# A long convolution and a soft mixture of experts in one kernel: the transform's first stage in 60 and 30 columns, its spectra stored by frequency, and a step's work put in another order

## The chip, the cores and the metric

The kernel runs on one core of one Trainium2 chip. The metric is device time in microseconds, the median of several executions. Times inside the kernel come from one execution that was recorded by the hardware profiler.

## The reference

All data is float32. `x` holds 8 sequences of 5696 tokens by 128 channels, `h` one filter of the same length. The first block is a causal convolution per channel by a Fourier transform of twice the length; the second block is a soft mixture of experts on the 45568 tokens that come out.

```python
Xf = np.fft.rfft(x, n=2*S, axis=1); Hf = np.fft.rfft(h, n=2*S, axis=0)
y = np.fft.irfft(Xf * Hf[None], n=2*S, axis=1)[:, :S, :].reshape(B*S, D)
logits = y @ phi                                  # 32 slots: 8 experts of 4
d = np.exp(logits - logits.max(0)); d /= d.sum(0) + 1e-9
slot_input = (d.T @ y).reshape(8, 4, 128)
slot_out[e] = np.maximum(slot_input[e] @ w1[e], 0) @ w2[e]
c = np.exp(logits - logits.max(1, keepdims=True)); c /= c.sum(1, keepdims=True) + 1e-9
out = c @ slot_out
```

## The kernel before, in words

The transform is split as 90 times 64 (N1 = 90, N2 = 64). A sequence is 89 rows (R1) of 64 tokens. For the filter and then each of the 8 sequences (g = 0 for the filter, 9 in all) the kernel walks through 8 steps (NJ); step c handles four tokens of the first half of each row and the four that mirror them, so there are 72 steps (NA) in which new data is transformed. All the work of all stages is put in one sequence of steps t, written out by hand; each engine, and SP, which issues nearly all DMAs, runs its own instructions in just that order.

**First stage.** `load_x` brings a step's tokens to a tile `xc` (two DMAs, 80 and 9 rows, in pieces of 2 KB); three such tiles are in rotation. `fold` adds or subtracts the mirrored tokens on POOL (L202; component 0 is the sum, 1 the difference). `stage_a(t, comp)` multiplies each of these by a table of 90 frequencies, spread over 128 columns: one matmul for the real and one for the imaginary part (L213), each into a PSUM bank, each copied by ACT into a tile `fst` (L215). Two DMAs of 45 frequencies each write `fst` to the spectrum `f` in DRAM (L219), whose layout is (half, token n, frequency q, re/im, channel), so in pieces of 1 KB. A step has four such matmuls and four such DMAs. The program's float32 matmul shows as two records in the profile.

**Second stage and back.** A unit is four of the 45 frequency rows (the last unit of a sequence is one); 12 units to a sequence, one in an odd step t and two in an even one. `load_g` reads a unit's spectra into a tile `gt` (L237; 128 rows of 4 KB). `stage_b1` transforms them over the 64 tokens into the PSUM tile `bt` (L251; two banks, one buffer); DVE multiplies by the filter's spectrum there (L269, L278); `stage_b2` transforms back into the PSUM tile `bz` (L293; two banks), ACT copies it (L298), SP writes it to `z` in DRAM (L301). `slot_b` runs `stage_b1` of a fresh unit and then `stage_b2` of the unit before it.

**Tokens and experts.** Every second step a pair T begins: `load_pair` reads `z` into the one tile `zc` (L329, five DMAs, rows of 16 KB), at the start of the even step before the pair's own. In the odd step `stage_c1` does the last stage of the inverse transform (L348) with `stage_c4` (L414 to L430) between its halves, and later `stage_c5` and `softmax`; in the even step come `stage_c2` (transposes, L376), `stage_c6`, `stage_c3` (logits, L385), `dispatch` (L461) and `column_max`. `pair(lag)` says which pair's stage falls in step t. The units of a sequence begin 9 steps, its pairs 27 steps after its first step.

**Rings.** All stages but b take their PSUM banks from one ring of four (`bank()`); a bank comes free when ACT or DVE has copied it. The other four banks are `bt` and `bz`. SP issues its DMAs in program order and waits at each until its data and its buffer are ready.

Order of an even step before: `load_pair`, `prefetch(t + 1)`, `load_x(t + 3)`, `stage_a(t, 0)`, fold, `dispatch`, unit, c2, c6, `stage_a(t, 1)`, fold, c3, unit, `column_max`. Order of an odd one: `prefetch(t + 1)`, `load_x(t + 3)`, `stage_a(t, 0)`, fold, c1 with c4, unit, c5, `stage_a(t, 1)`, fold, softmax. At the first step of a sequence `prefetch` comes later, after the middle unit.

After step 72 the first stage is over, and w1 is loaded; after the units end, `front` is closed and the last pairs run with eight banks. Then come the experts and the product with the output weights.

Of the kernel before, what the change touches and what calls it, by code (L numbers as in the profile page):

```python
# [10 lines left out]
F32 = mybir.dt.float32  # L11
AF = mybir.ActivationFunctionType
# [8 lines left out]
    return [(0, 64, 32, 1)] + left  # L21


def transform_tables(S, N1, N2, CH, X0, F0, F1):

# [16 lines left out]
    i1 = np.stack([np.cos(a0), -np.sin(a0), -np.cos(a0)], 1)  # L44
    NP = N1 // 2
    part = s1
    s1 = np.zeros((P, 3, P))
    for a, p in enumerate((F0, F1)):
        s1[X0:X0 + R1, :, p:p + NP] = part[:, :, a * NP:(a + 1) * NP]
    part = i1[np.arange(N1).reshape(2, NP).T.reshape(-1)]  # L50
    i1 = np.zeros((P, 3, N2))
    for r, n, p, step in z_blocks(N1):
# [23 lines left out]
def kernel(  # L76
# [25 lines left out]
    P = 128  # L102
# [15 lines left out]
    NQ = NJ // 2  # L118
    assert S == R1 * N2 and R1 == N1 - 1 and D == P and CH == Q == 4
    SPLIT = R1 // 16 * 16  # L120
    X0, F0, F1 = 20, 6, 82
    ctx.enter_context(tc.manual_schedule())

    t_s1, t_i1, t_w, t_v, t_turn = [
        nc.inline_tensor(t, f"tab_{n}").ap()
        for n, t in zip(("s1", "i1", "w", "v", "turn"), transform_tables(S, N1, N2, CH, X0, F0, F1))]
    fd = [nc.dram_tensor(f"f_{g}", (2, N2, NP, 2, D), F32, kind="Internal").ap() for g in range(B + 1)]
    zd = [nc.dram_tensor(f"z_{b}", (NP, 2 * N2, 2, D), F32, kind="Internal").ap() for b in range(B)]
    cd = nc.dram_tensor("c_t", (P, B * NQ, Q, 2, MH), F32, kind="Internal").ap()

# [28 lines left out]
    apool = lead.enter_context(tc.tile_pool(name="apool", bufs=2, side="right"))  # L159
    bpool = front.enter_context(tc.tile_pool(name="bpool", bufs=1))  # L160

    s1 = apool.tile([P, 3, P], F32, name="s1", tag="s1", bufs=1)
    wt = fconst.tile([P, NP, HP], F32, name="wt")
    vt = fconst.tile([P, NU, 2, HP], F32, name="vt")
    turn = fconst.tile([P, 2, NW, 2, 2], F32, name="turn")
# [3 lines left out]
    def bank():  # L169
        rings.append(rings.pop(0))  # L170
        return rings[-1].tile([P, 512], F32, name="bank", tag="bank")


    xs = {}
    xf = [apool.tile([P, CH, D], F32, name=f"x{i}", tag=f"x{i}", bufs=1) for i in range(2)]
    xcs = [apool.tile([P, 2, CH, D], F32, name=f"xc{i}", tag=f"xc{i}", bufs=1) for i in range(3)]
    for t_ in xcs:
        nc.vector.memset(t_[:, :, :, :], 0.0)

    def load_x(c):  # L180
        if c >= (B + 1) * NJ:
            return
        g, j = divmod(c, NJ)
        src = (h if g == 0 else x[g - 1]).rearrange("(a n) d -> a n d", n=N2)
        t_ = xcs[c % len(xcs)]
        gap = N2 - CH * (2 * j + 1)
        for r in (slice(0, SPLIT), slice(SPLIT, R1)):
            v = src[r, CH * j:CH * (j + 1), :]
            v = bass.AP(tensor=v.tensor, offset=v.offset,
                        ap=[v.ap[0], [gap * D, 2], [1, CH * D]])  # L190
            nc.sync.dma_start(
                out=t_[X0 + r.start:X0 + r.stop, :, :, :].rearrange("p s n d -> p s (n d)"), in_=v)
        xs[c] = t_

    folded = {}

    def fold(c, comp):
        if c not in xs:
            return
        t_ = xs.pop(c) if comp else xs[c]  # L200
        y_ = xf[comp]
        nc.gpsimd.tensor_tensor(out=y_[:, :, :], in0=t_[:, 0, :, :], in1=t_[:, 1, ::-1, :],  # L202
                                op=AL.subtract if comp else AL.add)
        folded[(c, comp)] = y_

    def stage_a(c, comp):
        g, j = divmod(c, NJ)
        src = folded.pop((c, comp))
        tab = (0, 1) if comp == 0 else (1, 2)
        st = apool.tile([P, CH, 2, D], F32, name="fst", tag="fst", bufs=5)  # L210
        for G in range(2):
            p = bank()
            nc.tensor.matmul(p[:, :], s1[:, tab[G], :],  # L213
                             src[:, :, :].rearrange("p n d -> p (n d)"), start=True, stop=True)
            nc.scalar.activation(st[:, :, G, :],  # L215
                                 p[:, :].rearrange("p (n d) -> p n d", d=D), AF.Copy)
        n0 = comp * HALF + CH * j
        for a, p in enumerate((F0, F1)):
            nc.sync.dma_start(  # L219
                out=fd[g][a, n0:n0 + CH, :, :, :].rearrange("n q c d -> q n (c d)"),  # L220
                in_=st[p:p + NP, :, :, :].rearrange("k n c d -> k n (c d)"))


    gs, prods = {}, {}

# [5 lines left out]
    def load_g(u):  # L231
        if u >= (B + 1) * NW:
            return
        g, w, us = parts(u)
        n = sum(k for _, k in us)
        t_ = bpool.tile([P, 4, 2, D], F32, name="gt", tag="gt", bufs=3)
        nc.sync.dma_start(  # L237
            out=t_[:, 0:n, :, :].rearrange("p q c d -> p (q c d)"),
            in_=fd[g].rearrange("a r q c d -> (a r) (q c d)")[:, 8 * w * D:(8 * w + 2 * n) * D])
        gs[u] = t_  # L240

    def stage_b1(u, share):
        g, w, us = parts(u)
        t_ = gs.pop(u)
        tag = "bz" if g == 0 and w % 2 else "bt"
        bt = bps.tile([P, 2, 2, 2 * D], F32, name="bt", tag=tag)
        for o, (i, n) in enumerate(us):
            for a in range(2):
# [9 lines left out]
        else:  # L258
            pv = bt[r, :, 0, :].rearrange("p a (c d) -> p a c d", c=2)
        k = 2 * m  # L260
        pi = bpool.tile([P, 4, 2, D], F32, name="p", tag="pi", bufs=2)
        for p_, H_ in ((pi[r, 0:k, :, :], turn[:, 1] if g == 0 else Hi), (pv, turn[:, 0] if g == 0 else Hr)):
            if g:
                h_ = H_[r, w].rearrange("p a o d -> p (a o) d") if m == 2 else H_[r, w, :, 0]
# [17 lines left out]
    def stage_b2(u):  # L282
        g, w, us = parts(u)
        if g == 0:
            return
        m = len(us)
        y_ = prods.pop(u)
        bz = bps.tile([P, 2, 2, 2 * D], F32, name="bz", tag="bz")
        for o, (i, n) in enumerate(us):
            for q in range(n):  # L290
                r = slice(q * HP, (q + 1) * HP)
                for a in range(2):
                    nc.tensor.matmul(bz[a * HP:(a + 1) * HP, q, o, :], vt[r, i, a, :],  # L293
                                     y_[r, a * m + o, :, :].rearrange("p c d -> p (c d)"),
                                     start=True, stop=True)
        n = us[0][1]
        st = bpool.tile([P, 2, 2, 2 * D], F32, name="zst", tag="zst", bufs=3)
        nc.scalar.activation(st[:, 0:m, 0:n, :].rearrange("p o q x -> p q o x"),  # L298
                             bz[:, 0:n, 0:m, :], AF.Copy)
        k = m * n  # L300
        nc.sync.dma_start(  # L301
            out=zd[g - 1][4 * w:4 * w + k, :, :, :].rearrange("q r c d -> r q (c d)"),
            in_=st[:, :, :, :].rearrange("p o q x -> p (o q) x")[:, 0:k, :])
# [243 lines left out]

    load_x(0)
    nc.scalar.dma_start(out=s1[:, :, :], in_=t_s1)
    for c in range(1, 3):  # L550
        load_x(c)
    nc.sync.dma_start(out=wt[:, :, :], in_=t_w)
    nc.sync.dma_start(out=vt[:, :, :, :], in_=t_v)
    nc.scalar.dma_start(out=phi[:, :], in_=moe_phi)
# [2 lines left out]
    for comp in range(2):  # L557
        fold(0, comp)
    wait_b2 = []

    for t in range(last_front + 1):
        us = list(units(t))

        def pair(lag):
            T, half = divmod(t - LAG_C - lag, 2)
            return T if half == 0 and 0 <= T < NT else None
# [4 lines left out]
                load_g(queue[loaded][0])  # L571
                loaded += 1

        turns = {2: (1, 3), 1: (2,)}.get(len(us), ())

        def slot_b(place=None):
            if place is not None and place not in turns:
                return
            fresh = bool(us)
            if fresh:  # L580
                u = us.pop(0)
                stage_b1(u, t < LAG_C or t >= NA)
                wait_b2.append(u)
            if len(wait_b2) > fresh:
                stage_b2(wait_b2.pop(0))

        if pair(-1) is not None:
            load_pair(pair(-1))
        if t % NJ:
            prefetch(t + 1)  # L590
        if t < NA:
            load_x(t + 3)
            stage_a(t, 0)
            fold(t + 1, 0)
        if pair(3) is not None:
            dispatch(pair(3))
        if t < last_front:
            slot_b(1)
        T, U = pair(0), pair(2)
        if t == last_front:  # L600
            assert T is None and U is None
            slot_b()
            slot_b()
            stage_c2(pair(1))
            slot_b()
            assert not us and not wait_b2
            V = pair(1)
            stage_c6(V - 2)
            stage_c3(V)
            column_max(V)  # L610
            break
        rows = (lambda: None) if U is None else (lambda: stage_c4(U))
        after = None
        if T is not None:
            after = stage_c1(T, rows)
        else:
            rows()
        if pair(1) is not None:
            stage_c2(pair(1))
        if pair(5) is not None:  # L620
            stage_c6(pair(5))
        if after:
            after()
        slot_b(2)
        if t % NJ == 0:
            prefetch(t + 1)
        if U is not None:
            stage_c5(U)
        if t < NA:
            stage_a(t, 1)  # L630
            fold(t + 1, 1)
        if pair(1) is not None:
            stage_c3(pair(1))
        slot_b(3)
        if pair(1) is not None:
            column_max(pair(1))
        if U is not None:
            softmax(U)
        if t == NA:
            lead.close()  # L640
            wts = inner.enter_context(tc.tile_pool(name="wts", bufs=1, side="right"))
# [221 lines left out]
```

## Time and profile before

| | |
|---|---|
| median of 6 runs | 898.47 us (895.01 to 903.22) |
| profiled execution, its time | 900.75 us |
| its span | 899.0 us |
| granted TensorE clock, mean | 0.949 |
| busy: PE, DVE, ACT, POOL | 808.3, 644.6, 480.9, 405.3 us |
| DMA moved | 272.44 MB in 156967 packets, mean 303 GB/s |
| DMA packets of the main queue | 90.3% of 16 engines' span |

Windows of the profile give each engine's busy time in a stretch of the span. A DMA share near 1.00 says that the time that all packets took, summed, is that of 16 engines busy all the time; packets overlap a little, so it can be above 1. The chain is the work that ended last, followed back: the engine and line named at each step is the one that all later work waited for.

### The profile page before, as it was taken

Reading aid. Unit: us, or ns where it says so; the run is one execution under the profiler, and the core shown is the slowest. Engines: PE = TensorE matmul, PEld = TensorE weight load, DVE = VectorE, ACT = ScalarE, POOL = GpSimd, SP = SyncE. Lnnn points to the kernel's source line nnn. Section 1 sums busy time; section 2 is a strip of 40 time slices with the busy share of each in tenths; the row PEclk is TensorE's granted clock in tenths of the full one; section 3 lists DMA queues with packets and bytes.
Section 4 is the critical chain, followed back from the end, with each engine's and each line's share of the span. In section 5 each row is a group of like instructions: output and inputs, shape, how many; then the busy total and the mean of one; then the engine's idle time right before and its main releaser. Section 6 shows DMA issues by size and latency. Waiting matters only on the chain.

```text
span 899.0 us, 19379 instructions
## 1 busy us (share of the span) xinstructions
PE 808.3 (90%) x7220; PEld 423.3 (47%) x7220; DVE 644.6 (72%) x928; ACT 480.9 (53%) x888; POOL 405.3 (45%) x385
## 2 busy tenths in 40 slices
PE   6959888789999999999999999999988877978893
PEld 2323334344445444544455555444544444445783
DVE  3039776676878888888888888777787987873542
ACT  4624344455655665666665666656653444683441
POOL 4624333244555555555555555555533343681000
PEclk9979999999999999999999999999999998988865
DMA  9989999999999999999999999999987986770898
GB/s 291 265 248 333 291 324 334 338 331 311 296 319 330 331 307 322 332 313 316 327 318 315 323 324 318 311 308 320 314 282 245 324 283 243 295 279 17 308 406 329
DMA packets 156967, 272.44 MB, mean 303 GB/s; under 512 B 12182, under 2 KB 114838, under 8 KB 153733
## 3 DMA queue, kind: packets, MB, share of 16 engines
q1 hardware_dynamic: 156299, 270.85, 90.3%
q8 instruction: 58, 0.95, 0.4%
q10 hardware_dynamic: 576, 0.36, 0.2%
q14 instruction: 34, 0.28, 0.1%
HBM read 142.86 MB, written 128.21 MB: 302 GB/s over the span
## 4 chain that ended last, share of the span: by engine, by line
PE 72%; DMA 17%; issue 3%; SPq 2%; DVE 2%; ACT 2%; POOL 1%; DVEq 0%; ACTq 0%; POOLq 0%
PE bank L213 25%; PE bank L348 12%; PE bt L251 11%; PE bz L293 8%; DMA gt<-f 5%; PE bank L376 5%; DMA out_dram<-o 4%; PE bank L461 3%; DMA zc<-z 3%; PE bank L385 2%; PE bank L437 2%; PE bank L414 2%; DMA f<-fst 1%; PE bank L485 1%; SPq L329 1%
## 5 line engine op out<-in xcount | busy, mean ns | idle before, releaser
L202 POOL TENSOR_TENSOR x<-xc 128x512 f32<-128x512 f32 x144 | 183.2, 1274 | 240.4 <-PE bank L213 183.0
L213 PE MATMUL bank<-x,s 128*128 128x512 f32 x576 | 276.3, 616 | 9.4 <-POOL x L202 9.3
L215 ACT ACTIVATE fst<-bank 128x512 f32<-128x512 f32 x288 | 171.6, 597 | 94.6 <-PE bank L213 79.6
L298 ACT ACTIVATE zst<-bz 128x1024 f32<-128x1024 f32 x96 | 93.3, 972 | 192.1 <-PE bz L293 172.4
L269 DVE TENSOR_TENSOR p<-bt,Hi 128x1024 f32<-128x1024 f32 x96 | 113.0, 1177 | 103.3 <-PE bt L251 102.9
L213 PEld LDWEIGHTS bank<-x,s 128*128 128x128 f32 x576 | 102.7, 193 | 127.9 <-issue 94.6
L251 PE MATMUL bt<-gt,wt 64*64 64x256 f32 x1620 | 116.7, 396 | 34.6 <-DMA gt<-f 17.4
L348 PE MATMUL bank<-zc,i 128*64 128x512 f32 x480 | 118.5, 617 | 7.6 <-DMA zc<-z 5.4
L278 DVE TENSOR_TENSOR yf<-bt,p 128x512 f32<-128x512 f32 x192 | 119.4, 663 | 3.3
L269 DVE TENSOR_TENSOR bt<-bt,Hr 128x1024 f32<-128x1024 f32 x96 | 113.0, 1178 | 0.0
L251 PEld LDWEIGHTS bt<-gt,wt 64*64 64x64 f32 x1620 | 55.3, 134 | 111.7 <-issue 58.2
L293 PE MATMUL bz<-yf,vt 64*64 64x256 f32 x1440 | 102.4, 382 | 0.0
L367 POOL TENSOR_TENSOR y<-y,op 128x512 f32<-128x512 f32 x64 | 77.4, 1210 | 7.9 <-DVE op L353 5.2
L293 PEld LDWEIGHTS bz<-yf,vt 64*64 64x64 f32 x1440 | 60.6, 135 | 21.9 <-issue 0.6
L367 POOL TENSOR_TENSOR y<-y,om 128x512 f32<-128x512 f32 x54 | 64.0, 1185 | 2.1
L348 PEld LDWEIGHTS bank<-zc,i 128*64 128x64 f32 x480 | 30.3, 138 | 69.1 <-issue 48.6
L422 POOL MEMSET dt<- 64x8 f32 x32 | 3.4, 107 | 123.0 <-issue 63.1
L376 PE MATMUL bank<-ident,y 109*128 109x109 f32 x512 | 57.7, 268 | 0.7 <-DVE y L367 0.7
L376 PEld LDWEIGHTS bank<-ident,y 109*128 109x128 f32 x512 | 51.2, 146 | 12.3 <-POOL L L450 6.6
L378 ACT ACTIVATE yt<-bank 128x360 f32<-128x360 f32 x128 | 50.1, 481 | 1.4 <-PE bank L376 1.4
L269 DVE TENSOR_TENSOR p<-bt,turn 128x1024 f32<-128x1024 f32 (+1 forms) x12 | 14.1, 1173 | 51.0 <-PE bt L251 50.9
L816 PE MATMUL op<-so,cT 32*128 32x128 f32 x704 | 45.8, 373 | 5.2 <-ACT o L825 4.7
(97 smaller groups left out, 856.3 us busy)
## 6 DMA issues: line engine op xcount, KB each, us to landing
f<-fst SPq DMA_DIRECT2D x288, 180.0 KB
gt<-f SPq DMA_DIRECT2D x99, 512.0 KB
z<-zst SPq DMA_DIRECT2D x88, 512.0 KB
zc<-z SPq DMA_DIRECT2D x30, 1024.0 KB
xc<-in_x_dram SPq DMA_DIRECT2D x64, 320.0 KB
out_dram<-o SPq DMA_DIRECT2D x16, 1024.0 KB
zc<-z SPq DMA_DIRECT2D x90, 128.0 KB
out_dram<-o SPq DMA_DIRECT2D x8, 768.0 KB
```

The lines of the kernel that those rows point to most:

```text
L202: nc.gpsimd.tensor_tensor(out=y_[:, :, :], in0=t_[:, 0, :, :], in1=t_[:, 1, ::-1, :], op=AL.subtract if comp else AL.add)
L213: nc.tensor.matmul(p[:, :], s1[:, tab[G], :], src[:, :, :].rearrange("p n d -> p (n d)"), start=True, stop=True)
L215: nc.scalar.activation(st[:, :, G, :], p[:, :].rearrange("p (n d) -> p n d", d=D), AF.Copy)
L251: nc.tensor.matmul(bt[q * HP:(q + 1) * HP, a, o, :], wt[r, 2 * i + q, :], t_[r, 2 * o + q, :, :].rearrange("p c d -> p (c d)"), start=True ...
L269: nc.vector.tensor_tensor(out=p_, in0=pv, in1=h_, op=AL.mult)
L278: eng.tensor_tensor(out=y_[r, 0:k, c, :], in0=pv[:, :, c, :], in1=pi[r, 0:k, 1 - c, :], op=op_)
L293: nc.tensor.matmul(bz[a * HP:(a + 1) * HP, q, o, :], vt[r, i, a, :], y_[r, a * m + o, :, :].rearrange("p c d -> p (c d)"), start=True, sto ...
L298: nc.scalar.activation(st[:, 0:m, 0:n, :].rearrange("p o q x -> p q o x"), bz[:, 0:n, 0:m, :], AF.Copy)
L348: nc.tensor.matmul(p[h_ * HP:(h_ + 1) * HP, :], i1[0:kr, tab, :], t_[0:kr, h_, o, :, q, :], start=True, stop=True)
L367: eng.tensor_tensor(out=part_, in0=part(v, 0), in1=o_[:, :, :], op=sign)
L376: nc.tensor.transpose(p[:, i * TR:(i + 1) * TR], ys[T][0:TR, k * CH + i, 0:D], ident[0:TR, 0:TR])
L378: nc.scalar.activation(yt[:, k * CH:(k + 1) * CH, :, :], of_tokens(p), AF.Copy)
```

## The change

The first stage's 90 frequencies, now ordered by q and half, are cut into 60 and 30. `first_low(c)` computes the first 60 of both components of a step in one bank: two matmuls of 64 columns, one beside the other in the output partitions, for each of the real and imaginary parts. `first_high(c)`, in odd steps alone, computes the last 30 of both components of two steps: four matmuls of 32 columns in a bank, again for each part. Each result is copied and stored: two DMAs of 60 rows from `first_low`, four of 30 rows from `first_high`. The spectrum `f` is now laid out (frequency q, half, token n, re/im, channel), so that a store's pieces are 4 KB, 64 KB apart; `load_g` reads four q of 128 rows in pieces of 1 KB.

`load_x` loads two steps at a time in pieces of 4 KB, into two tiles of twice the size; the folded tiles are four instead of two. `bt` has two buffers, which take all of the four banks outside the ring; `stage_b2` takes two banks of the ring, copied by two ACT instructions. `gt` has four buffers (three before), `fst` four (five before), `pi` one (two before). The order of a step is now a string of letters:

```diff
-    fd = [... (2, N2, NP, 2, D) ...]
+    fd = [... (NP, 2, N2, 2, D) ...]
...
-    xf = [apool.tile([P, CH, D], F32, ...) for i in range(2)]
-    xcs = [apool.tile([P, 2, CH, D], F32, ...) for i in range(3)]
+    xf = [apool.tile([P, CH, D], F32, ...) for i in range(4)]
+    xcs = [apool.tile([P, 2, 2 * CH, D], F32, ...) for i in range(2)]
...
-    def stage_a(c, comp):
-        st = apool.tile([P, CH, 2, D], F32, name="fst", tag="fst", bufs=5)
+    def first_stage(tiles, width):
+        st = apool.tile([P, CH, 2, D], F32, name="fst", tag="fst", bufs=4)
         for G in range(2):
             p = bank()
-            nc.tensor.matmul(p[:, :], s1[:, tab[G], :],
-                             src[:, :, :].rearrange("p n d -> p (n d)"), start=True, stop=True)
+            for o, (c, comp) in enumerate(tiles):
+                k = slice(0, HP) if width == HP else slice(HP, HP + QP)
+                nc.tensor.matmul(p[o * width:(o + 1) * width, :], s1[:, comp + G, k],
+                                 folded[(c, comp)][:, :, :].rearrange("p n d -> p (n d)"),
+                                 start=True, stop=True)
             nc.scalar.activation(st[:, :, G, :],
                                  p[:, :].rearrange("p (n d) -> p n d", d=D), AF.Copy)
-        for a, p in enumerate((F0, F1)):
+        for o, (c, comp) in enumerate(tiles):
+            g, j = divmod(c, NJ)
+            n0 = comp * HALF + CH * j
+            k0, n = (0, N1A) if width == HP else (N1A, N1 - N1A)
             nc.sync.dma_start(
-                out=fd[g][a, n0:n0 + CH, :, :, :].rearrange("n q c d -> q n (c d)"),
-                in_=st[p:p + NP, :, :, :].rearrange("k n c d -> k n (c d)"))
+                out=fd[g].rearrange("q a r c d -> (q a) (r c d)")[k0:k0 + n, n0 * 2 * D:(n0 + CH) * 2 * D],
+                in_=st[o * width:o * width + n, :, :, :].rearrange("k n c d -> k (n c d)"))
+    def first_low(c):
+        first_stage([(c, comp) for comp in range(2)], HP)
+    def first_high(c):
+        both = [(c - 1 + i, comp) for i in range(2) for comp in range(2)]
+        first_stage(both, QP)
...
-        t_ = bpool.tile([P, 4, 2, D], F32, name="gt", tag="gt", bufs=3)
+        t_ = bpool.tile([P, 4, 2, D], F32, name="gt", tag="gt", bufs=4)
         nc.sync.dma_start(
-            out=t_[:, 0:n, :, :].rearrange("p q c d -> p (q c d)"),
-            in_=fd[g].rearrange("a r q c d -> (a r) (q c d)")[:, 8 * w * D:(8 * w + 2 * n) * D])
+            out=t_[:, 0:n, :, :].rearrange("p q c d -> p q (c d)"),
+            in_=fd[g][4 * w:4 * w + n, :, :, :, :].rearrange("q a r c d -> (a r) q (c d)"))
...
-        tag = "bz" if g == 0 and w % 2 else "bt"
+        tag = f"bt{u % 2}"
...
-        bz = bps.tile([P, 2, 2, 2 * D], F32, name="bz", tag="bz")
+        bz = [bank() for _ in range(us[0][1])]
...
-        nc.scalar.activation(st[:, 0:m, 0:n, :].rearrange("p o q x -> p q o x"),
-                             bz[:, 0:n, 0:m, :], AF.Copy)
+        for q in range(n):
+            nc.scalar.activation(st[:, 0:m, q, :],
+                                 bz[q][:, 0:m * 2 * D].rearrange("p (o x) -> p o x", o=m), AF.Copy)
...
+    ORDER_E, ORDER_O, XAHEAD = "XYf1wb5s", "zXfb26dPxb3m", 4
...
+            "z": lambda: load_pair(pair(-1)) if pair(-1) is not None else None,
+            "x": lambda: load_x(t + XAHEAD) if t < NA else None,
+            "P": lambda: prefetch(t + 2),
+            "X": lambda: first_low(t) if t < NA else None,
+            "Y": lambda: first_high(t) if t < NA and t % 2 else None,
+            "f": lambda: [fold(t + 1, comp) for comp in range(2)] if t < NA else None,
+            "d": lambda: dispatch(pair(3)) if pair(3) is not None else None,
+            "b": lambda: slot_b(),
...
+        for c_ in (ORDER_E if t % 2 else ORDER_O):
+            work_[c_]()
```

`1` is c1 with c4 between its halves and `w` its second part; 2, 6, 5 and 3 are c2, c6, c5 and c3; `m` is `column_max`, `s` softmax. So `ORDER_E` is that of odd steps t, `ORDER_O` that of even ones: all units' spectra of two steps and x of two steps are loaded in the middle of the even step.

## The prediction

> **What bounds the kernel now.** The page's busy line says PE 808.3 of 899.0 us, its queue line that packets fill 90.3% of 16 DMA engines. Two resources that close need stages told apart, so the windows came next:
>
> ```profile
> core 0: us, PE busy (x) PEld busy (x) DVE busy (x) ACT busy (x) POOL busy (x), PEclk, DMA share, GB/s
> 0.00:50.00 50.00, 35.91 (x76) 14.03 (x76) 7.24 (x8) 23.55 (x39) 27.14 (x28) 1.00 0.91 276
> 110.00:200.00 90.00, 78.40 (x640) 38.15 (x632) 62.11 (x71) 45.09 (x67) 32.05 (x26) 1.00 1.01 330
> 149.00:171.00 22.00, 17.06 (x127) 8.66 (x128) 13.23 (x18) 9.89 (x15) 6.93 (x6) 1.00 1.02 336
> 200.00:660.00 460.00, 456.28 (x4037) 227.18 (x4040) 371.33 (x535) 278.13 (x508) 251.00 (x234) 1.00 0.97 318
> ```
>
> From 200 to 660 us (steps 27 to 72, all stages running) PE is busy 456.28 of 460 us, DMA at 0.97. What a full DMA looks like stands in the row above: 1.02, 336 GB/s, while PE idles a fifth of the time. So the middle is bound by PE with DMA about 5% behind, and the lead from 110 us on by DMA. The chain, over a period of two steps in the middle, is PE without a gap:
>
> ```profile
> 415.87 1.91 PE bank L213 x4
> 417.78 1.87 PE bank L348 x8
> 419.64 0.59 PE bank L414 x4
> 420.23 1.87 PE bank L348 x8
> 422.10 1.04 PE bt L251 x16
> ...
> 424.14 3.43 PE bank L213 x8
> ...
> 432.59 1.81 PE bank L213 x4
> 434.40 0.74 PE bank L385 x8
> ```
>
> and in the lead it runs through loads and stores of the spectrum:
>
> ```profile
> 148.97 6.88 DMA gt<-f
> 155.86 4.78 DMA f<-fst
> 160.72 5.97 DMA gt<-f
> ```
>
> A batch of eight steps takes 85.5 us in the middle (starts of the x8 piece, 338.60 to 424.14). I work per batch; the middle has 460 / 85.5 = 5.4 of them, the DMA-bound part of the lead 90 to 150 us, taken as 2.
>
> **PE.** Removed: eight full matmuls per period, 3.43 + 1.81 + 1.91 = 7.15 us. Added: `first_low` twice, which is two pairs of 64 columns each; that is exactly the shape of L348 (128*64, 512 columns, x8), 1.87 us, so 3.74. And `first_high`, two groups of four 32-column matmuls. No such group with 512 columns is in the trace. The nearest row is L385, four of 32 columns side by side, 360 columns long, 0.74 us: scaled by length 1.05 us a group; from below, a group can't beat a full matmul's 3.43 / 4 = 0.86. I take 1.0, as fill and drain don't scale. Together 5.74; saved 1.4 a period (1.3 to 1.7), 5.6 a batch: PE's floor is 79.9 us (78.7 to 80.3).
>
> The Trainium skill ("TensorE: Matmul & The Clock Gate", Measured speedup vs the span model) speaks against part of this: four tiles packed in rows gave 3.07 times, not 4. By that, an estimate, a group costs 1.12 us, the two 0.25 us more a period than I take. The sum keeps the value scaled from L385's row, which is this kernel's own.
>
> **DMA.** The trace's packet records between 300 and 600 us have means of 50 ns (1 KB), 110 (2 KB), 204 (4 KB), 725 (16 KB); the commonest times are 46, 84, 159, 611. The rest sits on the first packets of a DMA on each engine, and mostly on loads: 45 ns a packet for `gt`, 26 for `xc`, 4 for stores. Per batch, in packets times ns:
> - before: xc 1424 x 110, f 5760 x 50, z 5760 x 50, gt 1408 x 204 + 128 x 50, zc 360 x 725, c 512 x 64, others 12 us: 1335 us, / 16 = 83.4, that is 0.975 of 85.5, as the window says.
> - xc in half the DMAs and 4 KB pieces: 712 x 159 plus half the excess (18) = 132 us instead of 157: -25.
> - f stored in 4 KB: 1440 x 159 plus the same excess (24) = 253 instead of 288: -35.
> - gt read in 1 KB: 5760 x 46 plus the excess. It belongs to a DMA's start, and there are as many DMAs of as many bytes, so 63 us: 328 instead of 294: +34. If it belonged to the packet (45 each), 524: +230.
>
> Sum -26, / 16 = -1.6: 81.8 us of packets a batch. At 1.02 that is 80.2 us, at 0.975 it is 83.9.
>
> A rule of the skill speaks against the stores. "DMA: Bandwidth & Descriptors", Latency and other measured facts, says that a row pitch of large powers of two slows HBM, 207 GB/s at 512 KiB; the new stores have 64 KB, below its table. By an estimate at 207 GB/s the 5.9 MB of f a batch would take 28 us instead of 16. The trace has a row for the pitch: `zc` is read in rows 64 KB apart, and 611 ns for 16 KB (27 GB/s an engine) is its commonest packet time; it shows no such loss, for reads.
>
> **What else moves.** ACT: six copies of `fst` instead of eight (0.60 each), but `zst` in two of 0.60 instead of one of 1.03: -1.2 + 0.5 a period, with ACT busy 278 of 460: nothing. DVE keeps 371 of 460, at most 0.88 of a batch of 79 us: nothing, but it is close behind. `bt` with two buffers takes away the 1.06 us "issue" gaps before L251 in the lead (two a period); there DMA is the bound, so what is late next is the spectra: nothing. `bz` in the ring: 25 banks a period pass through four instead of 21. The slowest release is `dispatch`'s bank, copied by DVE behind a unit's 3.8 us (2 x 1.22 + 2 x 0.69); four allocations and about 2.9 us of PE follow (a unit's two halves and L385), and in the step's order DVE is done before: nothing, at worst 0.5 us a period. `pi` has one buffer, written and read by DVE alone: nothing. `xc` for two steps at the start doubles the first load: +1 us.
>
> SP's order: an even step now issues zc (5 DMAs), two stores of f, z, c, then three gt and two xc, then z; an odd one six stores of f and one z. Behind the five big loads wait only the last z and the odd step's stores; `zst` has three buffers and `fst` four, one period's worth or more, so their lateness is covered by up to a period. The gt loads are issued some 8 us before the first is needed and take 6.7 from issue to landing now: covered, without much to spare. But demand is uneven: about 5.5 MB in the even step (zc 1.5, gt 1.6, z 1.0, xc 0.7, f 0.5, c 0.2) and 1.5 in the odd one, where 336 GB/s carry 3.5 in a step's 10.4 us. The 2.0 MB left over plus the odd step's 1.5 are 10.4 us of work: DMA just stays busy, if SP issues early enough. I take a share of 1.00: 81.8 us a batch, PE's floor being 1.9 below.
>
> **Sum.** Middle: (85.5 - 81.8) x 5.4 = -20 us. Lead: 2 batches x 1.6 = -3; the first 50 us run PE-bound (x48 of L213 in 23 us) at share 0.91, of which I give back 4 us, less 1 for the first load. The last 240 us keep their work. 900.75 - 26 = 874.7; the profiled execution stands 2.3 above the median: **872 us**. Ends of this case: PE's floor of 79.9 and a lead 12 better, 5.4 x 5.6 + 12 = 42: 856; share 0.975, 8.6 + 3: 887.
>
> **Rivals.**
> 1. *The bunched loads let DMA run dry.* In the odd step SP has only stores, which PE paces. If the share falls to 81.8 / 85.5 = 0.957, the middle gains nothing and PE waits instead, seen as DMA gt or zc on the chain: about 893 to 898. For it: share 0.97 now, with an order that spreads loads over both steps. Against it: the work left over from the even step fills the odd one, by the sum above.
> 2. *Slower: the 1 KB reads cost by the packet.* Place: gt<-f in the lead and the middle. Row: xc's packets of 2 KB carry 26 ns each. At 46 + 26 = 72, gt takes 415 us instead of 294: with -60 of the others +61, / 16 = +3.8: 87.2 a batch at share 1.00, which is +1.7 x 5.4 = 9, and +7.6 in the lead, where it counts whole: 915. At 45 ns it would be 94 a batch and over 960. It decides from about 21 ns a packet, where packets fill 85.5. Stores slowed by their pitch would act the same way. For it: loads show nearly all the excess. Against: within a DMA, packets after the first run at the commonest time.
> 3. *Four tiles don't run together*, so the change doesn't save PE time: `first_high` would cost 8 x 0.86 = 6.9 a period instead of 2, 3.5 more than before. L385's 0.74 us rules it out.
>
> **Numbers.** Forecast 0.62, all of it faster; rival 1 0.15 (0.06 faster, 0.09 same); rival 2 and its like 0.23, slower. Faster 0.68, same 0.09, slower 0.23; the line between is 0.5% (4.5 us), about what a measurement of this kernel can tell from no change. Range: 856, PE's floor, to 912, into the second rival; its far bound stays outside with most of its chance.
>
> **What the profile after would show.** L213 with 64 and 32 columns, near 3.7 + 2.0 us a period on PE; a batch near 82 us; DMA share at or above 1.00 from 200 to 660 us with about 330 GB/s, and PE there at some 0.97, its waits named gt, zc or a bank. The mean of 1 KB packets below 55 ns. The "issue" gaps before L251 gone. It would be wrong if the share between 200 and 660 us falls below 0.96, if 1 KB packets go over 65 ns or 4 KB stores far over 170, or if PE's time per batch doesn't drop by 5 us.

## The result and the profile after

The changed kernel takes 895.41 us (median) where the kernel before took 899.72 in the same comparison: a ratio of 0.9954, 95% interval 0.994 to 0.9967. That is 0.5% faster where 2.9% (872 us) was forecast: inside the stated range (856 to 912), but about a sixth of the gain. Its profiled execution took 897.89 us, span 896.1.

PE's relief came as worked out. The windows of the changed kernel, in the columns shown before:

```profile
core 0: us, PE busy (x) PEld busy (x) DVE busy (x) ACT busy (x) POOL busy (x), PEclk, DMA share, GB/s
0.00:50.00 50.00, 32.29 (x138) 8.65 (x138) 8.04 (x7) 16.69 (x27) 25.39 (x27) 1.00 0.85 270
110.00:200.00 90.00, 69.55 (x672) 28.48 (x664) 58.91 (x68) 35.39 (x63) 28.41 (x24) 0.94 1.00 312
200.00:660.00 460.00, 435.26 (x4450) 202.66 (x4444) 353.53 (x540) 259.35 (x536) 252.94 (x234) 1.00 0.98 322
```

PE's busy time between 200 and 660 us fell from 456.28 to 435.26, but it now idles 25 us there; DMA share rose only from 0.97 to 0.98. In the lead DMA moves 312 GB/s at share 1.00, where it was 330 at 1.01.

Where the time went, by the start of each pair's c1 (the first matmul of L348, now L367, in the trace): the first pair starts at 190.1 us instead of 180.9, so the lead lost 9. The 22 pairs from there take 466 us instead of 473.5, a gain of 7 where 20 was forecast: a batch is 84.7 us, not 82 (pairs 4 to 20; 85.8 before by this count). What follows gains 4 to 5 more, where nothing was forecast; no run takes that apart.

The lead's 9 us have two parts. The first unit of spectra reaches PE 1.7 us later than before (56.1 us instead of 54.4), and from there to the first pair it takes 134.0 us instead of 126.5. In the first part the chain before was PE alone, six steps in 23 us:

```profile
8.05 23.08 PE bank L213 x48
```

After the change the first fold starts 2.7 us later (9.46 instead of 6.73 us), and PE and POOL take turns, two steps in 8.9 us instead of 7.7, as `first_high` reads the folded tiles of two steps and POOL refills them behind it:

```profile
9.46 1.27 POOL x L208
10.78 7.60 PE bank L219 x32
19.59 3.72 POOL x L208 x3
23.36 3.91 PE bank L219 x22
```

The chain of the changed kernel, in the middle, says how PE's time turned into a wait:

```profile
414.01 0.43 PE bank L395 x4
414.44 6.91 DMA zc<-z
...
421.41 0.35 SPq L515
...
421.82 6.08 DMA gt<-f
427.90 0.04 issue
427.94 1.09 PE bt L269 x16
```

L515 is c's store in `stage_c6`. It doesn't need zc. The trace never shows more than eight of these DMAs between issue and landing, and each uses one of eight completion semaphores in turn, so a DMA is issued only once the eighth before it has landed; SP waits there, and all behind it waits. Here z's five DMAs, two stores of f and one of z hold all eight places. The chain runs from z's load, over c's store that had to wait for the first of z's DMAs to land, to the spectra that SP could issue only then, to PE.

The other half of the same picture is SP's own row of time (start, duration of issue, line, count):

```profile
462.13 0.35 SPq L515 DMA_DIRECT2D c_t<-cst  x1
462.70 3.47 SPq L255 DMA_DIRECT2D gt<-f  x3
466.26 0.86 SPq L196 DMA_DIRECT2D xc<-in_x_dram  x2
467.22 0.60 SPq L320 DMA_DIRECT2D z<-zst  x1
467.91 8.03 SPq L228 DMA_DIRECT2D f<-fst  x6
476.39 0.39 SPq L320 DMA_DIRECT2D z<-zst  x1
476.96 3.56 SPq L348 DMA_DIRECT2D zc<-z  x5
```

The six stores of f take SP 8.03 us: the last three, whose data are ready, go out only as two of the loads of spectra and one of x ahead of them land. SP's waits from 200 to 660 us add that up:

```profile
SPq L228 <- DMA gt<-f: 70.9, 50, 2.8
SPq L228 <- DMA xc<-in_x_dram: 33.6, 21, 2.1
SPq L515 <- DMA zc<-z: 30.8, 19, 3.4
```

Before the change the largest such wait of f's stores for a DMA was 35.0 us (for zc).

In the lead, where there is no z to load yet, the spectra of the next steps wait behind such stores:

```profile
103.89 2.56 SPq L255 DMA_DIRECT2D gt<-f  x3
106.55 1.16 SPq L196 DMA_DIRECT2D xc<-in_x_dram  x2
107.80 9.58 SPq L228 DMA_DIRECT2D f<-fst  x8
117.48 0.58 SPq L320 DMA_DIRECT2D z<-zst  x1
118.16 2.88 SPq L255 DMA_DIRECT2D gt<-f  x3
```

From 50 to 200 us f's stores wait 37.5 us for spectra to land (26 times).

### The profile page after: what moved, and what is told of

It is laid out like the page before. It is cut to its first block, busy times and chain, and to the rows that moved or that the text cites. A ratio compares the mean times of both kernels' runs of the same rounds, so it can differ in the third digit from the quotient of the medians.

```text
span 896.1 us, 20345 instructions
## 1 busy us (share of the span) xinstructions
PE 767.0 (86%) x7796; PEld 376.7 (42%) x7796; DVE 622.0 (69%) x927; ACT 441.1 (49%) x904; POOL 403.1 (45%) x385
## 3 DMA queue, kind: packets, MB, share of 16 engines
q8 instruction: 62, 1.02, 0.5%
## 4 chain that ended last, share of the span: by engine, by line
PE 43%; DMA 37%; DVE 10%; issue 3%; SPq 2%; POOL 2%; ACT 1%; DVEq 0%; POOLq 0%; ACTq 0%
DMA zc<-z 11%; DMA gt<-f 11%; PE bank L219 10%; PE bank L367 7%; PE bt L269 7%; DMA f<-fst 6%; PE bank L311 5%; PE bank L395 4%; DMA out_dram<-o 4%; DMA xc<-in_x_dram 3%; PE bank L480 2%; DVE yf L296 2%; DVE p L287 2%; DVE bt L287 2%; PE op L823 2%
## 5 line engine op out<-in xcount | busy, mean ns | idle before, releaser
L208 POOL TENSOR_TENSOR x<-xc 128x512 f32<-128x512 f32 x144 | 179.4, 1271 | 244.2 <-PE bank L219 224.9
L219 PE MATMUL bank<-x,s 128*32 128x512 f32 (+1 forms) x1152 | 219.1, 613 | 17.7 <-POOL x L208 17.0
L317 ACT ACTIVATE zst<-bank 128x512 f32<-128x512 f32 (+1 forms) x184 | 98.7, 586 | 203.9 <-PE bank L311 195.0
L222 ACT ACTIVATE fst<-bank 128x512 f32<-128x512 f32 x216 | 127.5, 598 | 115.1 <-PE bank L219 87.1
L367 PE MATMUL bank<-zc,i 128*64 128x512 f32 x480 | 117.5, 611 | 21.4 <-DMA zc<-z 13.9
L311 PE MATMUL bank<-yf,vt 64*64 64x256 f32 x1440 | 102.2, 388 | 25.0 <-DVE yf L296 24.7
L219 PEld LDWEIGHTS bank<-x,s 128*32 128x32 f32 (+1 forms) x1152 | 53.8, 124 | 149.9 <-issue 80.0
L311 PEld LDWEIGHTS bank<-yf,vt 64*64 64x64 f32 x1440 | 57.2, 136 | 55.3 <-issue 30.0
L372 DVE TENSOR_TENSOR y<-bank,y 128x512 f32<-128x512 f32 x32 | 22.1, 691 | 80.3 <-PE bank L367 80.1
L367 PEld LDWEIGHTS bank<-zc,i 128*64 128x64 f32 x480 | 31.8, 137 | 85.1 <-issue 50.4
L395 PE MATMUL bank<-ident,y 109*128 109x109 f32 x512 | 63.7, 275 | 0.7 <-DVE y L386 0.7
L395 PEld LDWEIGHTS bank<-ident,y 109*128 109x128 f32 x512 | 53.4, 149 | 16.6 <-issue 10.8
L441 POOL MEMSET dt<- 64x8 f32 x32 | 3.4, 106 | 111.7 <-issue 69.4
L287 DVE TENSOR_TENSOR p<-bt,turn 128x1024 f32<-128x1024 f32 (+1 forms) x12 | 14.2, 1180 | 56.1 <-PE bt L269 55.5
```

The source lines that it names most:

```text
L208: nc.gpsimd.tensor_tensor(out=y_[:, :, :], in0=t_[0], in1=t_[1], op=AL.subtract if comp else AL.add)
L219: nc.tensor.matmul(p[o * width:(o + 1) * width, :], s1[:, comp + G, k], folded[(c, comp)][:, :, :].rearrange("p n d -> p (n d)"), start=Tr ...
L222: nc.scalar.activation(st[:, :, G, :], p[:, :].rearrange("p (n d) -> p n d", d=D), AF.Copy)
L287: nc.vector.tensor_tensor(out=p_, in0=pv, in1=h_, op=AL.mult)
L311: nc.tensor.matmul(bz[q][a * HP:(a + 1) * HP, o * 2 * D:(o + 1) * 2 * D], vt[r, i, a, :], y_[r, a * m + o, :, :].rearrange("p c d -> p (c ...
L317: nc.scalar.activation(st[:, 0:m, q, :], bz[q][:, 0:m * 2 * D].rearrange("p (o x) -> p o x", o=m), AF.Copy)
```

## The experiments

Theories at the start: A, DMA was already nearly full in the middle, so relief of PE buys little; B, the new layout of f costs DMA what PE gained; C, not bytes but SP's order and its eight places bind. Theory D, named in e9, is C in the lead.

**e1: PE's relief alone.** The imaginary part of the difference is left out; its copy takes the real part's bank.

```diff
 # kernel before, stage_a
-            p = bank()
-            nc.tensor.matmul(p[:, :], s1[:, tab[G], :], ...)
+            if G == 0 or comp == 0:
+                p = bank()
+                nc.tensor.matmul(p[:, :], s1[:, tab[G], :], ...)
```

> The kernel before with three first-stage matmuls a step instead of four (the imaginary part of the difference is not computed; its copy takes the real part's bank again): PE's relief alone, 1.8 us a period of two steps, with the same ACT copies, DMAs and order. Theory A (the middle's DMA is already nearly full, so relief of PE buys little): 4 to 12 us faster than before, the DMA share between 200 and 660 us at 0.98 to 1.00, PE no longer without gaps. Theory B (the change's own DMAs, 4 KB stores and 1 KB loads, ate the gain): PE's relief pays in full here, 25 to 35 us faster, a batch of eight steps near 79 us.

Measured: 886.38 us, 0.986 of before (0.9815 to 0.9906), a batch of 83.6 us.

```profile
200.00:660.00 460.00, 431.29 (x4079) 219.68 (x4078) 377.63 (x555) 276.00 (x521) 256.60 (x238) 1.00 0.98 326
```

That is A's range at its upper end, or just above it: with the old order, the old layout and one buffer for `bt`, a quarter of the first stage's matmuls is worth 13 us, and then DMA is at 0.98 and PE idles 29 us. A "full" DMA is 0.98 in the middle, not 1.00. But relief alone also beat the whole change, so the change takes something back.

**e2: the layout alone.** The kernel before with the spectrum stored by frequency:

```diff
-    fd = [... (2, N2, NP, 2, D) ...]
+    fd = [... (NP, 2, N2, 2, D) ...]
-                out=fd[g][a, n0:n0 + CH, :, :, :].rearrange("n q c d -> q n (c d)"),
+                out=fd[g][:, a, n0:n0 + CH, :, :].rearrange("q n c d -> q (n c d)"),
```

> The kernel before with the spectrum stored by frequency, nothing else: stores of 45 rows in 4 KB pieces 128 KB apart, loads in 1 KB pieces. In this kernel 4 KB packets are nearly all stores of f, and 2 KB are x, so their means can be told apart. Theory A: within 4 us of before, a store's 4 KB packet well under 190 ns on the mean. Theory B: 8 to 20 us slower, most of it in the lead before 200 us; 4 KB packets over 190 ns or 1 KB over 55 ns.

Measured: 896.81 us, 1.0002 (0.9962 to 1.0042). In the middle 1 KB packets, half of them now loads, took 51.2 ns on the mean (50.2 before), 4 KB packets, nearly all stores, 184 ns. All packets of a batch come to 82.8 us, 1.1 less than before the change in the same count. B falls, and with it the forecast's second rival. The Trainium skill's rule on row pitches of large powers of two ("DMA: Bandwidth & Descriptors", Latency and other measured facts) does not bite here: the pitch in this run is 128 KB, below its table. In that row 207 GB/s at 512 KiB stands beside a full rate of 214, so the row itself shows hardly any loss at that pitch, and the forecast's 28 us were no price for it. The changed kernel's own pitch, 64 KB, also ran in e9: 181 ns for a 4 KB packet.

**e3 and e5: half the spectra, after and before.** Two of a unit's four frequency rows are loaded, the rest of the tile holds zeros; as many DMAs, 2.9 MB a batch less.

```diff
-        t_ = bpool.tile([P, 4, 2, D], F32, name="gt", ...)
+        t_ = gts[u % 4]          # u % 3 in e5; set to zero at the start
+        n = (n + 1) // 2
```

> The changed kernel with half of each unit's spectra loaded (two of four frequency rows; the other half of the tile holds zeros from the start): 2.9 MB a batch of 27 less, in as many DMAs. Theory A (bytes bound it): 25 to 45 us faster than the changed kernel, a batch near PE's 79 to 80 us, DMA share falling to 0.90 to 0.95. Rival C (not bytes but SP's order and the number of DMAs in flight bind it): under 12 us faster, share falling with the bytes to about 0.89.

> The kernel before with half of each unit's spectra loaded, as in e3: the control. Theory A (before, the middle is PE's; after, it is DMA's): the middle keeps its batch of 85.5 us within 0.5 us, only the lead and the steps after the first stage gain, so 3 to 15 us faster than before, against 38 in e3. Rival (DMA set the pace of the middle before, too): 25 us or more faster, as in e3.

Measured: e3 857.55 us, 0.9534 of before (0.9505 to 0.9564), 38 us faster than the changed kernel; e5 885.64 us, 0.9884 (0.9829 to 0.9938). From 300 to 600 us, e3 and then e5:

```profile
300.00:600.00 300.00, 298.58 (x3055) 137.82 (x3057) 241.19 (x373) 179.18 (x371) 176.24 (x165) 1.00 0.92 304
```

```profile
300.00:600.00 300.00, 300.00 (x2654) 149.44 (x2654) 245.51 (x353) 184.24 (x338) 167.06 (x155) 1.00 0.90 286
```

e3 is bound by PE again, a batch of 80.6 us: this is the floor, forecast at 79.9. e5's batch is 85.5, before the change 85.8. So the middle was PE's before and is DMA's after, as forecast. What DMA makes of it isn't bytes alone, though: e3 also shortens every wait for a landing.

**e4: x ahead of the spectra.** `ORDER_O = "zXfb26dxPb3m"`.

> The changed kernel with the load of x one place earlier, ahead of the three loads of spectra. If x waiting in SP's queue behind spectra that wait for the stores of the step before is what lengthens the lead: the first pair's start comes 4 to 8 us earlier (190 us now, 181 before the change) and the kernel is 4 to 8 us faster. If not (the lead is bound by bytes or by the stores): within 2 us.

Measured: 914.3 us, 1.0167 (1.0093 to 1.0242), the first pair at 204.6 us. Wrong, and the other way: it is not x that suffers behind the spectra; putting x ahead of them hurts.

**e6: padding.** 4 KB behind each pair of rows of f.

> The changed kernel with 4 KB of padding behind each frequency row pair of f, so that a store's pieces are 64 and 68 KB apart in turn instead of 64 always; loads are the same pieces. If the power-of-two pitch costs the stores something: 4 KB packets from 196 ns in the middle to under 185, and 3 to 8 us faster than the changed kernel. If not: packets within 4 ns, time within 3 us.

Measured: 915.2 us, 1.0202 (1.0164 to 1.024). 4 KB packets took 201 ns on the mean, 196 in the changed kernel. The test is confounded: with the padding a store's rows can't be written with one stride, and SP takes 0.83 us to issue one instead of 0.31 to 0.42 (medians, 300 to 600 us). With eight stores a period SP has 3.6 us more to do. So this padding doesn't help, and its own effect stays open; that SP's time is what costs is likely, but not shown.

**e8: x by step.** `load_x` as before the change, four tiles, `x` also in `ORDER_E`.

> The changed kernel with x loaded one step at a time again (pieces of 2 KB, four tiles of the same room as the two, issued in both steps, still four steps ahead). In the changed kernel x's packets cost about 173 us a batch by the remainder, 157 before. If the large x loads are dearer for themselves: packets 1 us a batch less, 4 to 9 us faster than the changed kernel, the first pair 2 to 5 us earlier. Rival (more DMAs for SP's eight places in flight, cost of x unchanged): 0 to 6 us slower.

Measured: 894.07 us, 0.9956 (0.9926 to 0.9987), the changed kernel's time; packets 82.8 us a batch instead of 83.4, the first pair at 185.8 us. Between the two expectations: the larger x loads save nothing.

**e9: the spectra loaded as before the change.**

```diff
-    ORDER_E, ORDER_O, XAHEAD = "XYf1wb5s", "zXfb26dPxb3m", 4
+    ORDER_E, ORDER_O, XAHEAD = "pXYf1wb5s", "zpXfb26gdxb3m", 4
```

> The changed kernel with the spectra loaded as before the change, one unit at the start of the even step and two at the start of the odd one, instead of three in the middle of the even step; x stays in pairs. Theory D (in the lead the bunched loads fill the eight DMAs that SP has in flight, so the stores of f behind them, which the next spectra need SP to pass first, are issued late): the first pair from 190 us to 181 to 185, 5 to 10 us faster than the changed kernel. Rival (the lead is longer because its packets are dearer): within 3 us.

Measured: 876.13 us, 0.976 (0.9729 to 0.9791), 19 us faster than the changed kernel, about twice what was expected. The first pair starts at 182.2 us, a batch is 82.4 us, packets 80.8 us a batch.

```profile
200.00:660.00 460.00, 445.28 (x4580) 207.02 (x4576) 365.89 (x562) 266.38 (x550) 260.41 (x243) 1.00 0.97 330
```

SP's time at the same place as above:

```profile
463.49 0.41 SPq L255 DMA_DIRECT2D gt<-f  x1
...
468.01 0.35 SPq L515 DMA_DIRECT2D c_t<-cst  x1
468.58 1.70 SPq L196 DMA_DIRECT2D xc<-in_x_dram  x2
470.37 0.38 SPq L320 DMA_DIRECT2D z<-zst  x1
471.24 1.74 SPq L255 DMA_DIRECT2D gt<-f  x2
473.07 5.20 SPq L228 DMA_DIRECT2D f<-fst  x6
```

The six stores take 5.20 us instead of 8.03, and the even step's spectra stand ahead of c's store. From 50 to 200 us f's stores wait 6.2 us for spectra, not 37.5. The same bytes, the same matmuls: 332 GB/s between 300 and 600 us where the changed kernel moved 323.

**e11: the change's place for the spectra, in the kernel before.** `prefetch(t + 2)` in the middle of the even step, four buffers, `pi` one.

> The kernel before with the spectra's loads bunched as in the change: three units in the middle of the even step, four buffers (one buffer for pi makes the room). Nothing of the first stage, the layout or x is changed. If the bunching itself costs what e9 won back: 10 to 20 us slower than before, the first pair 5 us or more later than 181. Rival (it costs only where PE is relieved, since the middle here is PE's): middle unchanged at 85.5 a batch, at most the lead's 5 us.

Measured: 908.03 us, 1.0106 (1.0038 to 1.0175). The first pair at 187.4 us instead of 180.9; the middle keeps 85.9 a batch (85.8 before). The rival is right on the middle. The lead loses 6.5 us without any other part of the change; from the first unit of spectra to the first pair it takes 133.5 us, nearly the changed kernel's 134.0.

**e12 and e13: bunched or late?** e12 has three loads in a row, but at the odd step's start; e13 spreads them, in the middle of the steps.

```diff
-    ... "XYf1wb5s", "zXfb26dPxb3m", 4
+    ... "PXYf1wb5s", "zXfb26gdxb3m", 4      # e12; P loads t + 1 alone in a sequence's last step
+    ... "XYf1wpb5s", "zXfb26dpgxb3m", 4     # e13
```

> The changed kernel with the same three loads bunched, but at the start of the odd step instead of the middle of the even one (the first step of a sequence loads its one unit in the middle). If three in a row are what costs: as the changed kernel, within 5 us, SP's six stores of f still taking 7 us or more to issue. If their place is (behind z's load and c, ahead of x's): 10 us or more faster, towards e9's 876.

> The changed kernel with the loads spread as in e9 (one unit in the even step, two in the odd one), but in the middle of each step, not at its start. If spreading is what helps: within 5 us of e9 (876). If the early place is: nearer the changed kernel, over 885.

Measured: e12 880.5 us, 0.979 (0.9725 to 0.9855); e13 930.99 us, 1.0357 (1.0293 to 1.042), the first pair at 216 us. Both first expectations are wrong: three in a row cost next to nothing, the place is what counts. In e12 the stretch from the first unit of spectra to the first pair is back at 127.6 us. In e13 the lead shows what a late place does; its chain:

```profile
112.03 0.65 SPq L255
...
112.77 8.52 DMA xc<-in_x_dram
...
121.35 4.87 DMA gt<-f
126.22 0.14 issue
126.36 1.99 PE bt L269 x16
```

In the lead a load of e13 is issued 5.5 us (median) before PE reaches its unit and lands after 5.3; in the changed kernel it is 8.8 and 6.9, in e9 8.1 and 7.3. In the middle, over all loads, it is 9.0 in e13, 9.3 in the changed kernel, 10.9 in e9, 12.4 in e12, and 11.6 before the change. The medians don't tell everything: in the lead e9's is shorter than the changed kernel's, and e9 is the faster.

**e10: both by step.** e8 and e9 together.

> The changed kernel with both the spectra (as e9) and x (as e8) loaded step by step: the change without its new order of loads. If e9's gain is the bunching of spectra and e8's 1 to 3 us adds: 871 to 876. Rival (24 DMAs a period instead of 22 fill SP's time again): over 878.

Measured: 880.44 us, 0.9808 (0.9735 to 0.9881). Its interval overlaps e9's (0.9729 to 0.9791): no further gain is shown. The number is the rival's; whether SP's time is the cause wasn't tested.

**e14, e17 and e18: what of the place it is.** Still open was whether time to the first use counts or what stands behind the loads in SP's queue. e14 keeps three loads in the even step, ahead of c2, c's store and `dispatch`: `"zXfbP26dxb3m"`. e17 is e9 with the even step's unit ahead of z: `"pzXfb26gdxb3m"`. e18 is e9 again.

> The changed kernel with the same three loads bunched in the even step, but right behind its first unit, ahead of c2, c's store and dispatch: some 3 us earlier in PE's order, still ahead of x and the stores of f. If the time from issue to use decides: 878 to 886, the shortest waits (a tenth of the loads) from 6.1 us to 8 or more from issue to use. If what stands behind them in SP's queue decides: within 5 us of the changed kernel (895).

> e9's order with the even step's one unit of spectra loaded ahead of z's five DMAs instead of behind them. In e9 nearly all of PE's idle time in the middle is put down to gt. If that load's place still ends last: 3 to 6 us faster than e18. If z, now later, takes over: within 2 us or slower.

> The kernel of e9 once more, as the neighbour of e17: 874 to 880, 0.973 to 0.980 of before.

Measured: e14 888.19 us, 0.9873 (0.9821 to 0.9925); e17 882.01, 0.9813 (0.9768 to 0.9859); e18 875.74, 0.9749 (0.9708 to 0.979). e14 lies between its two expectations. Its middle is mended, 82.5 us a batch instead of 84.7. SP still needs 7.04 us for the six stores:

```profile
473.13 1.96 SPq L255 DMA_DIRECT2D gt<-f  x3
475.19 0.39 SPq L515 DMA_DIRECT2D c_t<-cst  x1
475.67 0.85 SPq L196 DMA_DIRECT2D xc<-in_x_dram  x2
476.62 0.39 SPq L320 DMA_DIRECT2D z<-zst  x1
477.41 7.04 SPq L228 DMA_DIRECT2D f<-fst  x6
```

The first of the three loads waits for z to land in e14 too. But the first place that comes free then goes to c's store in the changed kernel, and the load follows 0.64 us after z's first landing (median of the periods from 200 to 660 us), 6.3 us before PE reaches it: PE waits for it in nearly every period. In e14 the load goes first, 0.02 us after that landing, and 7.3 us ahead of PE. These 0.6 us a period are 2.5 a batch; the batch is 2.2 shorter. e4 fits: there two loads of x go first as well, the load follows 2.87 us after the landing, and its batch is 86.2.

In the lead e14's first pair starts at 187.6 us, but one profile of this number says little: e9 and e18 are one kernel and have 182.2 and 185.1. Counted from the first unit of spectra to the first pair, the runs part in two: 134.0 us in the changed kernel, 133.5 in e11, 131.1 in e14 and 130.9 in e8, which load in the middle of the even step, against 126.5, 128.8, 127.6, 127.6 and 126.8 in e9, e18, e17, e12 and e10, which load earlier. In the changed kernel and in e9, e18, e17 and e12 bytes and packet times there are nearly the same (129.5 us of packets; 127.1, 129.6, 129.5 and 128.4), so it is not dearer packets: the DMA share of that time was 0.97 in the changed kernel and 1.00 to 1.02 in the four. So in the lead, too, it is the place. That it acts by the stores of f behind the loads is read from SP's lines and waits; no run moved those stores alone.

e17's batch is 82.4 us, as e18's 82.5: an earlier place for that one load brings nothing there. Its six runs (880.0 to 884.1) are all slower than e18's six (875.3 to 878.7). The 6 us lie behind the middle, from the 23rd pair's start on (243.3 us against 237.1), in part at a lower granted clock (0.88 against 0.93 from the 26th to the 29th pair); whether order or clock did it is open.

## Why the prediction was wrong

Right: what bound each stage (e5, e3), PE's saving (a batch of 80.6 us at the floor against 79.9 worked out; the two groups of 32 columns take 69.4 us in 36 periods, 0.96 us each, where 1.0 was taken), and that the new layout costs nothing (e2). The Trainium skill's 3.07 for four packed tiles ("TensorE: Matmul & The Clock Gate", Measured speedup vs the span model) gave an estimate of 1.12 us for such a group; the trace differs, and the measured 0.96 decides.

Wrong, by its own steps:
- **"The gt loads are issued some 8 us before the first is needed and take 6.7 from issue to landing now: covered."** This step failed, and with what it cost in the lead it is the largest. The sum put down no price for the moved loads. In the middle the first of three was issued 6.3 us before PE reached it, not 8, since SP could issue it only when z's load had landed and c's store had gone ahead of it. The place behind c's store was worth 2.2 us a batch (84.7 against e14's 82.5), 12 of the 20 us forecast for the middle.
- **The lead, forecast 6 us faster, lost 9.** Two terms failed. "Of which I give back 4 us" for the first 50 us: PE's relief bought nothing there, as PE then waited for POOL's folds, and the spectra came 1.7 us later. And the 1.6 us a batch of cheaper packets: from the first unit to the first pair the packets took 124.5 us before, 129.5 after, and no run that loads all spectra was shorter there than before (126.5). On top came the place of the loads, 5 to 7.5 us (134.0 against 126.5 to 128.8). The forecast had looked at the stores behind the loads and saw "`zst` has three buffers and `fst` four, one period's worth or more, so their lateness is covered". The buffers were not what mattered: SP itself stood still at those stores.
- **DMA's share of 1.00.** In the middle it reached 0.97 to 0.99 where DMA binds (the changed kernel, e1, e9). 81.8 us of packets at 0.98 are 83.5 a batch; the packets themselves came to 80.8 in e9 and to 83.4 in the changed kernel, and why they were slower there is open. With the loads moved forward the batch came near the forecast (82.4 in e9, 82.5 in e18 and e14), by two errors that partly cancel.
- **First rival.** It named the bunched loads and a price near the one measured ("about 893 to 898"), and the waits for gt and zc that it named stand on the chain. But it came to the price by a share that falls to 0.957; the share rose to 0.98. Bunching wasn't the cause either: e12 bunches and runs at 880.

With the spectra's loads left where they were, the kernel comes near the forecast: e9 and e18 ran in 876 us, 0.976 and 0.9749 of before, against 872. They beat both kernels. That the total is so near is partly luck: their middle gains the forecast 20 us (21 and 22), but the lead loses 1 to 4 where 6 were to be gained, and what follows the 22 pairs gains 7 where nothing was.

Left open: why e4, which moves the three loads behind two of x alone, costs as much as 19 us (its lead is 15 us longer than the changed kernel's; its SP lines fit the same account, but no run took it apart), the gain behind the 22 pairs, and the padding.

## What to carry to other kernels

Where one queue issues all DMAs in order and only so many are in flight, a load's place in that queue is part of its latency: look at what it stands behind, what that one waits for to land, and what stands behind it. "Issued early enough" has to be checked at the shortest distances and along the queue, not with a median latency. When PE is relieved, ask first how full the next resource really gets in that stage: a run of the old kernel that relieves PE alone (e1), one that relieves DMA alone (e5), and the new kernel with DMA relieved (e3) bracket the gain before any order is touched.

## What the runs showed of the hardware

A store of 60 rows in 4 KB pieces took SP 0.42 us to issue (median), and 0.84 where padding gave its rows two strides instead of one (e6); with eight stores a period that is a visible load on SP. Larger pieces did not make x's loads cheaper: x's 8 KB packets took 531 ns on the mean in the changed kernel, 66 ns a KB, where e8's 2 KB packets took 113, 57 a KB; with the spectra loaded by step e9's 8 KB packets took 416 (52 a KB) and e10's 2 KB packets 102 (51). And DMA's rate depended on the order alone: the same bytes and pieces went at 323 GB/s in the changed kernel and at 332 in e9, both at a share of 0.98 to 0.99.
